# Unpacking double-precision weights beside an attention loop: three stages in three steps, integer mantissas, and another start

## The chip, the cores and the metric

One core of one Trainium2 chip. The metric is device time in microseconds (us) of one execution. The engines are PE (TensorE: matmuls), PEld (its weight loads), DVE (VectorE), ACT (ScalarE), POOL (GpSimd) and SP (SyncE, which starts the transfers). In these traces an engine works through its own instructions in program order (the prediction shows ACT standing for 3.77 us with a ready exponential behind it), and engines wait for one another by semaphores. "Granted clock" is the share of full speed that the chip's throttle gave PE.

## The reference

Attention in which a query sees only the keys with the same hash, then a feed-forward block with a squared ReLU:

```python
q_bits = (np.einsum('bhsd,dk->bhsk', q, proj) > 0)       # 4 x 8 heads, 768 tokens, 64 features, 6 bits
mask   = q_bucket[:, :, :, None] == k_bucket[:, :, None, :]
scores = np.where(mask, scale * q @ k.T, -1e9)
attn   = exp(scores - max); attn /= sum(attn) + 1e-9
x      = (attn @ v) as (3072, 512)
out    = np.maximum(x @ w_in, 0)**2 @ w_out              # w_in 512 x 2048, w_out 2048 x 512
```

The two weight matrices reach the kernel as 64-bit floating-point numbers. The kernel takes them apart with integer operations and puts fp32 numbers together.

## The kernel before

There are two stages. The attention stage works on 16 pairs of heads; a pair takes six steps, here called k0 to k5, one for each block of 128 keys. In each step PE makes scores in two sets of PSUM banks, ACT takes the exponential (which frees the banks), DVE adds the exponentials up, and PE multiplies the exponentials of an earlier step by the values ("attend"). Between these stands the preparation of the next pair: DVE transposes the queries (k1) and the keys (k2), PE hashes both (k3), ACT takes the signs (k3, k4). The product stage is the feed-forward block. The weights, in 32 pieces of 128 x 512, are converted during the attention stage, two pieces for each pair.

```python
    def part_weight(i):                                    # before
        high = raws[i][:, :, 1]
        nc.vector.tensor_scalar(out=power, in0=high, scalar1=20, scalar2=0x7FF,
            op0=ALU.logical_shift_right, op1=ALU.bitwise_and)
        nc.vector.tensor_scalar(out=top, in0=high, scalar1=3, scalar2=0x7FFFFF,
            op0=ALU.logical_shift_left, op1=ALU.bitwise_and)
        nc.scalar.activation(out=small, in_=power, func=ACTF.Relu, bias=excess)
        nc.scalar.activation(out=power, in_=small, func=ACTF.Copy, scale=2.0**23)
        nc.scalar.activation(out=one, in_=top, func=ACTF.Copy, scale=2.0**-23, bias=1.0)
    def round_weight(i): ...                               # three DVE operations over two tensors
    ...
        w_early.setdefault(u + (second if close else 2 * second), []).append((part_weight, i))
        w_steps.setdefault(u + (2 if close else SB - 1) + second, []).append((round_weight, i))
    ...
        for u in range(len(steps) + 1):
            for f, i in w_early.get(u, ()): f(i)           # ahead of the step's work
            add_up(*steps[u - 1])
            score(pr, kt)                                  # PE scores, then ACT's exponentials
            # ... spread, hash_bits, signs, weigh, attend, sum_up, normalize
            # ... features: DVE transposes q (k1) or k (k2) of the next pair
            for f, i in w_steps.get(u, ()): f(i)           # after it
```

So the two DVE operations and the three ACT operations on a piece are issued ahead of the step's exponentials.

## Time and profile before

| | before |
|---|---|
| median time | 1004.67 us (three runs) |
| span of the profiled run | 1002.8 us |
| first score matmul / first product matmul | 14.9 / 417.3 us |
| period of an undisturbed pair, hash to hash | 24.35 to 24.37 us |
| DVE / ACT busy in one pair | 17.4 / 17.2 us |

The lines on which the reading rests are shown inside the prediction below. One line of the page's fifth part (the costliest groups) belongs with them. Its columns are line, engine, operation, what is written and read with shapes, count, then busy us and mean ns, then the idle time of the engine just before this group and what ended it:

```profile
L147 ACT ACTIVATE small<-power,excess 128x512 uint8<-128x512 uint32 x32 | 23.1, 722 | 66.0 <-DVE power L137 65.9
```

The 23.1 us of work are not remarkable; the 66.0 us that ACT stood before it are. Idle time of an engine costs nothing unless something needed stands behind it, and here the exponentials do.

### The profile page before, as it was taken

What the parts mean: (1) busy time and instruction counts of PE and PEld (TensorE: products, weight loads), DVE (VectorE), ACT (ScalarE), POOL (GpSimd) and SP (SyncE); (2) the same over time, 40 slices, a digit from 0 to 9 for tenths busy, and PEclk for the clock granted to TensorE, in tenths of its full rate; (3) what the DMA queues carried; (4) which work ended last, traced back from release to release, by engine and by line L of the source; (5) the groups of instructions that cost most, each with busy time, mean ns of one, the idle gap of its engine ahead of it and who ended that gap; (6) DMA issues with size and microseconds to landing.
All of it is one profiled execution on the core that took longest, in us unless ns stands there. A gap on an engine that the chain in (4) does not pass through costs nothing.

```text
span 1002.8 us, 12978 instructions
## 1 busy us (share of the span) xinstructions
PE 941.5 (94%) x5166; PEld 656.1 (65%) x5166; DVE 555.6 (55%) x1074; ACT 390.0 (39%) x721; POOL 6.0 (1%) x22
## 2 busy tenths in 40 slices
PE   5888888888888888999999999999999999999998
PEld 2333333333333333588888888888888888888886
DVE  2677767777777777697028604840583068306600
ACT  5777667676766666232013102310221022002200
POOL 2000000000000000000000000000000000000000
PEclk8999999999999999999999999999999999999999
DMA  9454444454545521001022102210221021100000
GB/s 188 93 118 106 105 105 107 105 143 110 148 106 124 129 74 38 17 0 42 22 69 63 58 22 69 64 58 22 84 63 42 22 87 61 53 25 8 1 22 24
DMA packets 121155, 70.12 MB, mean 70 GB/s; under 512 B 99328, under 2 KB 104448, under 8 KB 121088
## 3 DMA queue, kind: packets, MB, share of 16 engines
q1 hardware_dynamic: 121024, 69.22, 26.4%
q8 instruction: 42, 0.69, 0.3%
q14 instruction: 25, 0.20, 0.1%
q0 software_dynamic: 64, 0.00, 0.0%
HBM read 54.53 MB, written 14.68 MB: 69 GB/s over the span
## 4 chain that ended last, share of the span: by engine, by line
PE 61%; DVE 1%; ACT 1%; issue 0%; DVEq 0%; ACTq 0%
PE acc L579 58%; PE xo L367 2%; PE st L339 1%; PE tot L385 0%; ACT e L344 0%; ACT small L147 0%; ACT power L148 0%; DVE flip L391 0%; ACT one L149 0%; DVE feat L281 0%; PE hash L294 0%; DVE power L137 0%; DVE w_out L166 0%; DVE one L163 0%; DVE power L159 0%
## 5 line engine op out<-in xcount | busy, mean ns | idle before, releaser
L579 PE MATMUL acc<-x,w_in 128*128 128x256 f32 x768 | 174.8, 379 | 0.0
L579 PE MATMUL acc<-w_out,g 128*128 128x256 f32 x768 | 168.7, 379 | 0.0
L344 ACT ACTIVATE e<-st 128x1024 f32<-128x1024 f32 x192 | 145.1, 806 | 54.4 <-PE st L339 52.5
L579 PEld LDWEIGHTS acc<-w_out,g 128*128 128x128 f32 x768 | 145.9, 190 | 19.8
L579 PEld LDWEIGHTS acc<-x,w_in 128*128 128x128 f32 x768 | 145.8, 190 | 19.8
L339 PE MATMUL st<-feat,feat 64*128 64x512 f32 (+1 forms) x768 | 154.9, 494 | 0.0
L367 PE MATMUL xo<-e,v_nat 128*64 128x512 f32 (+1 forms) x768 | 148.2, 507 | 4.6 <-DVE x_t L422 3.3
L579 PE MATMUL acc<-t_x,s_in 128*128 128x256 f32 x576 | 132.2, 379 | 0.0
L579 PE MATMUL acc<-t_out,gs 128*128 128x256 f32 x576 | 126.3, 379 | 0.0
L579 PEld LDWEIGHTS acc<-t_out,gs 128*128 128x128 f32 x576 | 109.5, 190 | 14.9
L579 PEld LDWEIGHTS acc<-t_x,s_in 128*128 128x128 f32 x576 | 109.4, 190 | 14.9
L367 PEld LDWEIGHTS xo<-e,v_nat 128*64 128x64 f32 x768 | 47.8, 139 | 95.7 <-issue 84.6
L339 PE MATMUL st<-bits,bits 64*128 64x256 bf16 (+1 forms) x384 | 65.0, 332 | 45.1 <-ACT e L344 40.1
L357 DVE TENSOR_TENSOR total<-total,e 128x1536 f32<-128x1536 f32 x48 | 84.3, 1757 | 32.7 <-ACT e L344 32.6
L339 PEld LDWEIGHTS <-bits 64*128 64x128 bf16 x384 | 20.6, 94 | 109.8 <-issue 108.7
L703 DVE TENSOR_TENSOR o<-acc,two 128x256 f32<-128x256 f32 x12 | 5.1, 424 | 156.7 <-PE acc L579 156.7
L339 PEld LDWEIGHTS st<-feat,feat 64*128 64x128 f32 x768 | 68.6, 193 | 34.5 <-issue 32.2
L673 DVE SCALAR_TENSOR_TENSOR g<-h 128x256 f32<-128x256 f32 x192 | 77.3, 423 | 4.9
L586 ACT COPY two<-acc 128x256 f32<-128x256 f32 x60 | 22.3, 372 | 143.4 <-PE acc L579 142.0
L304 ACT ACTIVATE bits<-hash,lifts 32x384 bf16<-32x384 f32 x120 | 68.6, 572 | 4.5 <-PE hash L294 2.7
L147 ACT ACTIVATE small<-power,excess 128x512 uint8<-128x512 uint32 x32 | 23.1, 722 | 66.0 <-DVE power L137 65.9
L672 DVE TENSOR_TENSOR h<-acc,two 128x256 f32<-128x256 f32 x48 | 20.3, 424 | 51.1 <-PE acc L579 51.1
(87 smaller groups left out, 626.4 us busy)
## 6 DMA issues: line engine op xcount, KB each, us to landing
raw<-in_moe_w_in_dram SPq DMA_DIRECT2D x16, 512.0 KB, 4.2
raw<-in_moe_w_out_dram SPq DMA_DIRECT2D x16, 512.0 KB, 3.7
v_nat<-in_v_dram SPq DMA_DIRECT2D x16, 384.0 KB, 3.9
x_all<-x_t SPq DMA_DIRECT2D x16, 384.0 KB, 2.7
x<-x_all SPq DMA_DIRECT2D x6, 1024.0 KB, 5.1
out_dram<-o SPq DMA_DIRECT2D x24, 256.0 KB, 2.0
raw_qk<-in_k_dram SPq DMA_DIRECT2D x16, 384.0 KB, 3.1
raw_qk<-in_q_dram SPq DMA_DIRECT2D x16, 384.0 KB, 3.3
```

The source lines that it names most:

```text
L147: nc.scalar.activation(out=small, in_=power, func=ACTF.Relu, bias=excess)
L304: nc.scalar.activation(out=t[h * D:h * D + NR_B, c * HS:(c + 1) * HS], in_=hashed[pr][h][at, 0:HS], func=ACTF.Sign, scale=HUGE, bias=lifts ...
L339: nc.tensor.matmul(out=st[:, h, 0:hi - lo], lhsT=src[pr, 1][rows, key], rhs=src[pr, 0][rows, lo:hi], start=first, stop=not first,)
L344: nc.scalar.activation(out=e[:, :, lo:hi], in_=st[:, :, 0:hi - lo], func=ACTF.Exp, scale=scale)
L357: nc.vector.tensor_tensor(out=totals[pr], in0=in0, in1=weights[pr, kt][:, :, 0:S], op=ALU.add)
L367: nc.tensor.matmul(out=xo[h * D:(h + 1) * D, lo:hi], lhsT=nat[pr, "v_nat"][:, h, kt * D:(kt + 1) * D], rhs=weights[pr, kt][:, h, lo:hi], s ...
L579: nc.tensor.matmul(out=acc[to], lhsT=a(i), rhs=b(i), start=first and i == 0, stop=last and i == n - 1, skip_group_check=True,)
L586: nc.scalar.copy(out=t, in_=acc[of])
L672: nc.vector.tensor_tensor(out=h, in0=one, in1=two, op=ALU.add)
L673: nc.vector.scalar_tensor_tensor(out=out, in0=h, scalar=0.0, in1=h, op0=ALU.max, op1=ALU.mult)
L703: nc.vector.tensor_tensor(out=out, in0=one, in1=two, op=ALU.add)
```

## The change

The intent is that ACT never waits for DVE. A piece now goes through three stages in three different steps: DVE takes it apart, ACT places the exponent in a later step and after that step's exponential, and DVE rounds in a step later still. The mantissa stays an integer until it is rounded, which saves one ACT operation on each piece. The sums over weights (all but the first) and over the first chunk of x move to the heads of steps. At the very start the first pair's key bits are made by comparisons on DVE instead of signs on ACT.

```diff
-        nc.vector.tensor_scalar(out=top, in0=high, scalar1=3, scalar2=0x7FFFFF, logical_shift_left, bitwise_and)
+        nc.vector.tensor_scalar(out=top, in0=high, scalar1=0xFFFFF, scalar2=0x100000, bitwise_and, bitwise_or)
+        parts[i] = power, top
+    def place_power(i):
         nc.scalar.activation(out=small, in_=power, func=ACTF.Relu, bias=excess)
         nc.scalar.activation(out=power, in_=small, func=ACTF.Copy, scale=2.0**23)
-        nc.scalar.activation(out=one, in_=top, func=ACTF.Copy, scale=2.0**-23, bias=1.0)
 ...  # round_weight: low * 2**-32 + top as integers; the last operation also scales by 2**-20
-        w_early ... part_weight;  w_steps ... round_weight
+        if i < 2:    at = i, 3 + i, 4 + i, 5 + i
+        elif second: at = max(u - 3, SB - 1), u + 1, u + 2, u + 4
+        else:        at = max(u - SB - 1, ...), u - 1, u, u + 3
+        for f, n in zip((load_weight, part_weight, place_power, round_weight), at):
+            w_steps.setdefault(n, []).append((f, i))
 ...  # sums_in, all but the first: from the end of a k3 to the head of a k0; sums_x: from the end of step 66 to the head of step 36
-        for w in (1, 0): signs(0, w)
-        weigh(0)
+        signs(0, 0)
+        first_keys()      # four comparisons and one multiply-add on DVE
```

(Argument lists are shortened and cuts are marked by "...".)

More of the change, by code (lines that the diff above doesn't have):

```diff
@@ L133, in part_weight @@
         power = p_w.tile([P, PIECE], U32, name="power")
-        small = p_w.tile([P, PIECE], U8, name="small")
-        one = p_w.tile([P, PIECE], FP32, name="one")
-        top = one.bitcast(U32)
+        top = p_w.tile([P, PIECE], U32, name="top")
         nc.vector.tensor_scalar(
@@ L141, in part_weight @@
         nc.vector.tensor_scalar(
-            out=top, in0=high, scalar1=3, scalar2=0x7FFFFF,
-            op0=ALU.logical_shift_left, op1=ALU.bitwise_and,
-        )
+            out=top, in0=high, scalar1=0xFFFFF, scalar2=0x100000,
+            op0=ALU.bitwise_and, op1=ALU.bitwise_or,
+        )
+        parts[i] = power, top
+    def place_power(i):
+        if i not in parts:
+            return
+        power = parts[i][0]
+        small = p_w.tile([P, PIECE], U8, name="small")
         nc.scalar.activation(out=small, in_=power, func=ACTF.Relu, bias=excess)
         nc.scalar.activation(out=power, in_=small, func=ACTF.Copy, scale=2.0**23)
-        nc.scalar.activation(out=one, in_=top, func=ACTF.Copy, scale=2.0**-23, bias=1.0)
-        parts[i] = power, one
     def round_weight(i):
@@ L157, in round_weight @@
         low, high = raw[:, :, 0], raw[:, :, 1]
-        power, one = parts.pop(i)
+        power, top = parts.pop(i)
         nc.vector.scalar_tensor_tensor(
@@ L162, in round_weight @@
         )
+        one = top.bitcast(FP32)
         nc.vector.scalar_tensor_tensor(
-            out=one, in0=low, scalar=2.0**-52, in1=one, op0=ALU.mult, op1=ALU.add,
+            out=one, in0=low, scalar=2.0**-32, in1=top, op0=ALU.mult, op1=ALU.add,
         )
-        nc.vector.tensor_tensor(
-            out=pieces[i][3], in0=one, in1=power.bitcast(FP32), op=ALU.mult
+        nc.vector.scalar_tensor_tensor(
+            out=pieces[i][3], in0=one, scalar=2.0**-20, in1=power.bitcast(FP32),
+            op0=ALU.mult, op1=ALU.mult,
         )
@@ L181 @@
     lifts = const.tile([P, 1], FP32, name="lifts")
+    spans = const.tile([P, 1], FP32, name="spans")
+    bases = const.tile([P, 1], FP32, name="bases")
     excess = const.tile([P, 1], FP32, name="excess")
@@ L196, in constants @@
             nc.gpsimd.dma_start(out=projs[h * D:(h + 1) * D, 0:N], in_=proj)
-        for t in (gains, lifts):
+        for t in (gains, lifts, spans, bases):
             nc.vector.memset(t, 0.0)
@@ L203, in constants @@
             nc.vector.memset(gains[r:r + N], FAR / 2)
+            nc.vector.memset(bases[r:r + N + 1], -FAR / 2 * N)
+            nc.vector.memset(bases[r:r + N], -FAR / 2)
+            nc.vector.memset(spans[r:r + N], FAR)
         for r in range(0, P, NR_B):
@@ L307, in signs, with first_keys @@
                 )
+    def first_keys():
+        bits[0, 1] = t = all_bits[0][1]
+        for c in range(2):
+            at = slice((2 + c) * NR_B, (3 + c) * NR_B)
+            for h in range(2):
+                nc.vector.tensor_scalar(
+                    out=t[h * D:h * D + NR_B, c * HS:(c + 1) * HS], in0=hashed[0][h][at, 0:HS],
+                    scalar1=0.0, scalar2=None, op0=ALU.is_gt,
+                )
+        nc.vector.tensor_scalar(
+            out=t, in0=t, scalar1=spans, scalar2=bases, op0=ALU.mult, op1=ALU.add
+        )
     def weigh(pr):
@@ L464 @@
         u, second = i // 2 * SB, i % 2
-        last = i // 2 == NP - 1
-        w_steps.setdefault(max(u - SB + (SB - 1) * second, i), []).append((load_weight, i))
         if i < 2:
-            u = SB // 2
-        close = last or i < 2
-        w_early.setdefault(u + (second if close else 2 * second), []).append((part_weight, i))
-        w_steps.setdefault(u + (2 if close else SB - 1) + second, []).append((round_weight, i))
-    W_IN = len(pieces) // 4 * SB + 1
-    for r in range(NR):
-        w_steps.setdefault(W_IN + r * SB + 2, []).append((sums_in, r))
-    X_0 = 5 * PB * SB // 2
+            at = i, 3 + i, 4 + i, 5 + i
+        elif second:
+            at = max(u - 3, SB - 1), u + 1, u + 2, u + 4
+        else:
+            at = max(u - SB - 1, (0, 2, SB)[i // 2] if i < 6 else 0), u - 1, u, u + 3
+        for f, n in zip((load_weight, part_weight, place_power, round_weight), at):
+            w_steps.setdefault(n, []).append((f, i))
+    W_IN = len(pieces) // 4 * SB - 1
+    for r in range(NR):
+        if r == 0:
+            w_steps.setdefault(W_IN + 4, []).append((sums_in, r))
+        else:
+            w_early.setdefault(W_IN + 1 + r * SB, []).append((sums_in, r))
+    X_0 = (PB + 1) * SB
     xs = {}
@@ L502 @@
         hash_bits(0, (st[:, 0], st[:, 1]))
-        for w in (1, 0):
-            signs(0, w)
-        weigh(0)
+        signs(0, 0)
+        first_keys()
         for u in range(len(steps) + 1):
@@ L509 @@
                 f(i)
+            if u == X_0 + SB:
+                sums_x(0)
             if 1 <= u <= len(steps):
@@ L549 @@
                 load_x(0)
-            if u == X_0 + SB:
-                sums_x(0)
         first.close()
```

## The prediction

> **What bounds the kernel now.** I read the page first: its engine shares and its 40 slices, then the list of waits, then the timeline of one repeat.
>
> ```profile
> PE 941.5 (94%) x5166; PEld 656.1 (65%) x5166; DVE 555.6 (55%) x1074; ACT 390.0 (39%) x721; POOL 6.0 (1%) x22
> ...
> PE   5888888888888888999999999999999999999998
> DVE  2677767777777777697028604840583068306600
> ACT  5777667676766666232013102310221022002200
> ```
>
> Two stages stand out. From slice 17 on (about 417 us, the first product matmul is at 417.3) PE has no gap; in the attention stage before it, it is eight tenths busy, while DVE and ACT stand at about seven. The change touches only the attention stage, so the last 1002.8 - 417.3 = 585.5 us should stay as they are, and the question is why PE idles in the first 417. The list of waits (engine and line, who it waited for, us in total, times, longest) answers:
>
> ```profile
> ACT small L147 <- DVE power L137: 65.9, 31, 6.3
> PE st L339 <- ACT e L344: 40.1, 18, 3.1
> PEld xo L367 <- DVE x_t L422: 10.2, 14, 3.0
> PE st L339 <- ACT bits L304: 4.9, 1, 4.9
> PE xo L367 <- DVE x_t L422: 3.3, 3, 2.6
> ```
>
> PE waits 18 times, 40.1 us, for an exponential, about once for each of the 16 head pairs. The first line hints at why the exponential is late: ACT itself has stood for 65.9 us before a weight-piece instruction. The timeline of one pair (start, duration, engine, line, what; in brackets the idle time before it) shows the order:
>
> ```profile
> 118.30 0.97 DVE L413 STREAM_TRANSPOSE recs<-tot 128x768 f32<-128x768 f32 x1
> 119.37 1.02 DVE L422 SCALAR_TENSOR_TENSOR x_t<-xo,recs 128x768 f32<-128x768 f32 x1
> 120.31 0.97 DVE L281 STREAM_TRANSPOSE feat<-q_nat 128x768 f32<-128x768 f32 x1
> 121.20 0.38 DVE L137 TENSOR_SCALAR power<-raw 128x512 uint32<-128x512 uint32 x1
> 121.62 0.72 ACT L147 ACTIVATE small<-power,excess 128x512 uint8<-128x512 uint32 x1 [3.77 <-DVE power L137]
> 122.38 0.63 ACT L148 ACTIVATE power<-small 128x512 uint32<-128x512 uint8 x1
> 122.91 0.61 ACT L149 ACTIVATE one<-one 128x512 f32<-128x512 uint32 x1
> 123.43 1.49 ACT L344 ACTIVATE e<-st 128x1024 f32<-128x1024 f32 x2
> 124.49 0.39 PE L339 MATMUL st<-bits,bits 64*128 64x512 bf16 x2 [2.52 <-ACT e L344]
> ```
>
> DVE comes to the piece's first operation only after the rounding of another piece, recs, x_t and the transposed queries. ACT meets the piece *ahead of* this step's exponential, stands 3.77 us, works 1.8 us, and only then starts the exponential that frees the score banks; PE is 2.52 us late. The scores had been ready since about 119.8 (they start at 118.54; with ACT idle the exponential follows 1.3 us later, as 116.34 does 115.04).
>
> **What the Trainium skill says.** "PSUM — Partial Sum Buffer", section Engine vs sequencer instructions, says that ScalarE and VectorE queues are strict first-in first-out. The lines above agree: a ready exponential stood 3.6 us behind a conversion. "TensorE: Matmul & The Clock Gate", Part 1, says that an idle PE falls to half its clock for a window of about 3.4 us. Here gaps of 2.5 us, shorter than the gap it warns of, do it sometimes:
>
> ```profile
> 100.14:124.49 24.35, 21.71 (x155) 8.72 (x155) 17.41 (x23) 17.17 (x27) 0.00 (x0) 1.00 0.48 108
> 124.49:150.41 25.92, 23.28 (x154) 9.13 (x154) 17.41 (x23) 17.27 (x27) 0.00 (x0) 0.93 0.45 102
> ```
>
> The columns after the length are the busy time of PE, PEld, DVE, ACT, POOL, then the granted clock. The same pair costs 1.57 us more at a mean clock of 0.93. "ScalarE: Activation LUTs", What ACT_TABLE_LOAD costs, gives 186 ns + 0.833 ns an element for an activation with immediates: 613 ns at 512 elements, and L149 takes 613 here. "VectorE: DVE Perf Modes", Mode 2×_2P, says that one-source fp32 operations in SBUF run at twice the rate of two-source ones: here 0.42 us for a TENSOR_SCALAR of 512 elements against 0.68 for a SCALAR_TENSOR_TENSOR.
>
> **The change, part by part.**
>
> *Busy time.* ACT loses the 32 activations of L149: 32 x 0.613 = 19.6 us. DVE keeps five operations for a piece of the same kinds and sizes (two of 0.42, three of 0.68; the last becomes a SCALAR_TENSOR_TENSOR, 0.684 instead of 0.692). None of this is on PE's path by itself.
>
> *Order.* I call the steps of a pair k0 to k5. The first piece of a pair is now taken apart on DVE at the end of the last pair's k5, placed on ACT after the exponential of k0, rounded at k3; the second at k1, k2 (after the exponential), k4. A walk through one pair, from the trace's durations with PE unhindered: k0 at 0; k1 at 4.60 (it has the total matmuls); k2 8.10; k3 11.27; k4 15.25 (hash matmuls, 0.81); k5 18.42; next pair 21.59. That is 6 x 3.17 (scores 1.72, attend 1.45) + 1.43 + 0.33 + 0.81.
> - ACT: an exponential starts 1.29 after its scores and may be up to 0.82 late before PE waits (PE follows its start by 1.06; 3.17 - 1.29 - 1.06 = 0.82). k0: exponential to 2.80, piece (0.72 + 0.63) to 4.15, next exponential due 5.89. k2: exponential to 10.90, piece to 12.25, next due 12.56. k3, k4: key and query signs of 2.33 each, as before; k5's exponential begins at 20.38, 0.67 late, inside the 0.82. No wait.
> - DVE at k1: without the rounding (which stood between 116.37 and 118.4), recs runs at 6.75 to 7.72 and x_t starts when attend ends, about 8.24, not 9.2 to 9.3 as now. The second piece's first operation ends at 10.5, before ACT is free at 10.90. x_t ends at 9.3, before the next attend at 9.82, so PE's small wait there goes too: k2 now takes 3.43 before the stall (118.54 to 121.97), 0.26 over 3.17. The sums of the x chunk move from k0 of a late pair, where they held x_t (PE waited 2.64), to the head of k0, where DVE has some 4 us free.
> - DVE at k3, k4: add and rounding 3.8 and, with weigh, 4.2 us against steps of 3.98 and 3.17; it catches up in k5 (total ready about 22.7, needed at 24.8).
>
> *Sum.* Of the 40.1 us: the start-up wait of 0.57 stays, and in the first pair (pieces in k3 and k4 beside both sign steps) I allow 1.2, for 38.3 saved. x_t: 14 x 0.26 + 2.6 = 6.2. Half clock: four pairs with 1.57, the last pair about 1.6, 7.9 together. Start: before the first score ACT does eight signs of 0.57 and PE waits 4.9; now four signs on ACT (2.3) beside four comparisons and one multiply-add on DVE (estimated 4 x 0.45 + 0.42 = 2.2 from DVE's 0.58 for 384 elements out of PSUM in flip and 0.42 for bits): 2.3 saved. Total 54.7, hence 950.
>
> **The rivals.**
> - *A new wait of PE for the keys' features.* DVE's second-step order is queries, piece, total, keys; by the walk the keys end at 13.35 and the second half of the hash needs them at 13.40. A DVE 0.3 us later costs 15 x 0.3 = 4.5 us. For it: no slack. Against: before, the stall hid it, and most of DVE's other work left these steps. I put in 3 us: 953.
> - *DVE becomes the bound.* It works 17.4 us a pair; with the four weight sums of 1.55 us in half the pairs, 19, against a period of 21.6. It binds only where k3 and k4 pile up: then the total or x_t would be late, perhaps 0.5 us a pair, 960.
> - *ACT is still late.* If pieces landed between signs and exponentials as in pair 0, 1.2 us a pair, 18 us, would stay: 970. The walk speaks against it, with 0.15 us of slack at k5.
> - *The loads are the hidden limit.* DMA is half busy and would have to bring the same bytes in 360 instead of 417 us; no PE or ACT wait names a load after the start, and q and k come two pairs ahead. Unlikely; 965 or more.
> - *Stage 1's saving is given back in the product stage.* PE has no gap there to fill or lose; against.
>
> **Range and chances.** With every wait gone and the full clock it would be about 947; with a quarter of the gain lost, 965. I say 953, from 947 to 963. Slower than 984.6 (2%) would need two thirds of the gain to vanish though the cause is plain in the trace: 0.96 for faster, 0.03 for same, 0.01 for slower.
>
> **What would show it.** In the changed profile: PE's wait for exponentials under 3 us; no long wait of ACT for DVE's power; the period of a pair 21.6 to 22 us against 24.36; granted clock 1.00 in every pair after the first; the first product matmul at 362 to 368 us; the stage behind it 585.5 us long. Waits of PE for feat (hash) or x_t would be the first rival; exponentials 0.8 us late after signs, the third. A stage two that is longer, or a pair period that stays above 23, would make the prediction wrong.

## The result

| | before | after |
|---|---|---|
| median time, same rounds | 1005.07 us | 959.44 us |
| ratio | | 0.9546 (95%: 0.9529 to 0.9562) |
| span of the profiled run | 1002.8 us | 956.8 us |
| first product matmul | 417.3 us | 370.7 us |
| product stage | 585.5 us | 586.1 us |
| period of an undisturbed pair | 24.36 us | 21.93 to 21.96 us |
| mean granted clock | 0.988 | 0.995 |

The time lies in the predicted range, 6.4 us above its centre. All of the gain is in the attention stage, which is 46.6 us shorter; the product stage is 0.6 us longer. The page of the changed kernel, its engine totals and slices:

```profile
PE 936.7 (98%) x5166; PEld 653.6 (68%) x5166; DVE 553.7 (58%) x1086; ACT 372.9 (39%) x685; POOL 6.0 (1%) x22
...
PE   5999999999999999999999999999999999999997
DVE  2677778778888886970287028702870187016600
ACT  4777777777777772320131013201320132013200
```

PE's eights have become nines from the second slice on. Three lines of the list of waits (engine and line, who it waited for, us in total, times, longest):

```profile
PE st L363 <- DVE bits L329: 5.4, 1, 5.4
PEld hash L304 <- DVE feat L291: 3.8, 14, 0.8
PE st L363 <- ACT e L368: 1.9, 2, 1.4
```

ACT's wait for DVE's exponents has gone from 65.9 to 0.3 us (one wait), and PE's wait for exponentials from 40.1 to 1.9 us: now ACT waits for PE's scores, 79 times and 89.5 us in all, as it should when PE is the bound. Two of the lines are new. At the start PE waits 5.4 us for DVE's key bits (before: 4.9 us for ACT's). And 14 times the weight load of the hash waits for DVE's transposed features. The timeline of one pair, around the place of the old stall (start, duration, engine, line, what, with the idle time before it in brackets):

```profile
133.01 1.02 DVE L446 SCALAR_TENSOR_TENSOR x_t<-xo,recs 128x768 f32<-128x768 f32 x1 [0.47 <-PE xo L391]
133.96 0.97 DVE L291 STREAM_TRANSPOSE feat<-q_nat 128x768 f32<-128x768 f32 x1
134.85 0.39 DVE L135 TENSOR_SCALAR power<-raw 128x512 uint32<-128x512 uint32 x1
135.48 1.75 DVE L381 TENSOR_TENSOR total<-e,e 128x1536 f32<-128x1536 f32 x1
135.60 0.72 ACT L152 ACTIVATE small<-power,excess 128x512 uint8<-128x512 uint32 x1
137.15 0.97 DVE L291 STREAM_TRANSPOSE feat<-k_nat 128x768 f32<-128x768 f32 x1
137.79 0.15 PEld L304 LDWEIGHTS hash<-feat,projs 64*32 64x32 f32 x8 [0.33 <-issue]
137.79 1.24 PE L304 MATMUL hash<-feat,projs 64*32 64x384 f32 x16
138.17 0.16 PEld L304 LDWEIGHTS hash<-feat,projs 64*32 64x32 f32 x8 [0.23 <-DVE feat L291]
138.96 1.51 PE L391 MATMUL xo<-e,v_nat 128*64 128x512 f32 x8
```

ACT takes the piece at once and then waits 0.38 us for the scores. The hash starts at 137.79 and the next work of PE at 138.96, 1.17 us later; before it was 0.80 (275.48 to 276.28 in a pair of the old trace). The weight loads of the hash in that old pair show the difference:

```profile
275.48 0.18 PEld L294 LDWEIGHTS hash<-feat,projs 64*32 64x32 f32 x16 [0.33 <-issue]
```

There all 16 loads went out within 0.18 us, and 8 of the 16 matmuls started within the first 0.06 us: the half for the queries and the half for the keys ran side by side. In the changed kernel 8 loads go out at 137.79 and 4 matmuls start in the first 0.06 us; the 8 loads of the key half follow only at 138.17, after DVE has written the keys' features (137.15 to 138.12). The halves run one after the other, and that is 0.36 us more. A whole pair in the changed kernel (after the length: busy time of PE, PEld, DVE, ACT, POOL, then the granted clock):

```profile
137.79:159.72 21.93, 21.93 (x156) 8.71 (x154) 19.52 (x28) 16.26 (x25) 0.00 (x0) 1.00 0.53 120
```

PE counts as busy for the whole period although it is 0.36 us longer than it need be: half of a hash is work too, and of the wait only the 0.23 us before the second weight loads show, as idle PEld. This pair also holds the sums of x; in an ordinary one (93.91 to 115.85) DVE is busy for 17.0 us, and in the fullest pair looked at (with a sum of weights) for 19.9. The clock is 1.00, and it is 1.00 over the whole stretch from 50 to 365 us.

### The profile page after: what moved, and what is told of

It reads as the page before. It is cut to its first block, busy times and chain, and to the rows that moved or that the text cites. A ratio compares the mean times of both kernels' runs of the same rounds, so it can differ in the third digit from the quotient of the medians.

```text
span 956.8 us, 12947 instructions
## 1 busy us (share of the span) xinstructions
PE 936.7 (98%) x5166; PEld 653.6 (68%) x5166; DVE 553.7 (58%) x1086; ACT 372.9 (39%) x685; POOL 6.0 (1%) x22
## 4 chain that ended last, share of the span: by engine, by line
PE 96%; DVE 1%; ACT 1%; DMA 0%; issue 0%; SPq 0%; DVEq 0%; ACTq 0%
PE acc L607 61%; PE st L363 17%; PE xo L391 14%; PE tot L409 2%; PE hash L304 2%; PE tot L433 1%; ACT bits L314 0%; ACT e L368 0%; DMA q_nat<-in_q_dram 0%; PE tp L281 0%; DVE bits L325 0%; DVE feat L291 0%; DVE total L381 0%; PE st L304 0%; DVE flip L415 0%
## 5 line engine op out<-in xcount | busy, mean ns | idle before, releaser
L368 ACT ACTIVATE e<-st 128x1024 f32<-128x1024 f32 x192 | 145.5, 810 | 90.0 <-PE st L363 89.5
L363 PE MATMUL st<-feat,feat 64*128 64x512 f32 (+1 forms) x768 | 151.7, 487 | 0.0
L391 PE MATMUL xo<-e,v_nat 128*64 128x512 f32 (+1 forms) x768 | 144.9, 498 | 0.2 <-DVE x_t L446 0.2
L607 PEld LDWEIGHTS acc<-t_out,gs 128*128 128x128 f32 x576 | 109.4, 190 | 14.9
L607 PEld LDWEIGHTS acc<-t_x,s_in 128*128 128x128 f32 x576 | 109.4, 190 | 14.9
L614 ACT COPY one<-acc 128x256 f32<-128x256 f32 x60 | 22.4, 373 | 67.3 <-PE acc L607 67.3
```

The source lines that it names most:

```text
L363: nc.tensor.matmul(out=st[:, h, 0:hi - lo], lhsT=src[pr, 1][rows, key], rhs=src[pr, 0][rows, lo:hi], start=first, stop=not first,)
L368: nc.scalar.activation(out=e[:, :, lo:hi], in_=st[:, :, 0:hi - lo], func=ACTF.Exp, scale=scale)
L391: nc.tensor.matmul(out=xo[h * D:(h + 1) * D, lo:hi], lhsT=nat[pr, "v_nat"][:, h, kt * D:(kt + 1) * D], rhs=weights[pr, kt][:, h, lo:hi], s ...
L607: nc.tensor.matmul(out=acc[to], lhsT=a(i), rhs=b(i), start=first and i == 0, stop=last and i == n - 1, skip_group_check=True,)
L614: nc.scalar.copy(out=t, in_=acc[of])
```

## The experiments

Eleven runs in three groups; the runs of a group share the runs of the kernel before (medians 1005.04, 1005.06 and 1005.66 us). The time of a group's kernels is compared with that of the changed kernel run again, 959.43 us. That run and the rest of the first group (a_banks, a_featk, a_both) were on one chip and the other two groups on another; the kernel before differs by 0.6 us between them. "Wait" and "period" are from the profile of each run.

| run | median us | ratio to before | period us | what it is |
|---|---|---|---|---|
| a_same | 959.43 | 0.954 | 21.94 | the changed kernel again |
| a_banks | 957.36 | 0.9517 | 21.94 | key hash of the first pair in its own PSUM banks |
| a_featk | 954.06 | 0.9487 | 21.58 | keys transposed before adding up |
| a_both | 950.75 | 0.9457 | 21.58 | both edits |
| a_start | 959.45 | 0.9527 | 21.94 | old start |
| a_arith | 959.64 | 0.953 | 21.94 | old arithmetic, three activations |
| a_sums | 960.47 | 0.9543 | 21.94 | sums in their old steps |
| a_round | 969.79 | 0.9633 | 22.65 | second rounding in its old place |
| b_place | 974.65 | 0.9683 | 22.65 | before, ACT's part of a piece after the exponential |
| b_ints | 995.60 | 0.9881 | 23.84 | before, new arithmetic only |
| a_best | 949.72 | 0.944 | 21.58 | a_both, first two pieces in other steps |

### a_same: the changed kernel again

No edit.

> The changed kernel once more, unaltered, as the base for the three beside it: 958 to 960 us, period of a pair 21.94 us (hash to hash), first score at about 15.4 us.

959.43 us (958.87 to 960.19), period 21.94. First score 15.55 us.

### b_place: only ACT's place in the order

```diff
-        nc.scalar.activation(...)  x3, inside part_weight
+    def place_weight(i): the same three activations
         w_early.setdefault(n, []).append((part_weight, i))
+        w_steps.setdefault(n, []).append((place_weight, i))    # same step, after the exponential
```

> The kernel before with one thing altered: ACT's three instructions on a piece are issued after the step's exponential instead of ahead of it; arithmetic, DVE's order and start as before. Theory (the exponential stood behind the piece in ACT's queue): PE's waits for exponentials fall from 40 us to under 5, the half clock goes, and the keys become what the hash waits for: period about 22.6, 968 to 974 us. Rival (ACT's freed time or the new steps are needed): 990 or more.

974.65 us: 31.0 us of the 45.6 come from this one edit, with the old arithmetic, the old start, and DVE's order of operations unchanged. Two of its waits:

```profile
PEld hash L302 <- DVE feat L289: 10.7, 14, 0.8
PE st L347 <- ACT e L352: 3.9, 3, 2.5
```

The exponentials' 40.1 us are down to 3.9 us, and the hash now waits for the features, by more than in the changed kernel (10.7 against 3.8 us). The time is 0.65 us above the range expected: the first pair's wait is 2.5 us here, and the pair with the sums of x lasts 25.19 us, 2.54 more than its neighbours, because those sums still hold x_t. These two pairs (the first lasts 25.49 us against 23.28 in the changed kernel) and the place of the rounding (a_round, 10.4 us) account for about 15.1 of the 15.2 us that still separate this run from the changed kernel.

### b_ints: only the arithmetic

```diff
-        nc.scalar.activation(out=one, in_=top, func=ACTF.Copy, scale=2.0**-23, bias=1.0)
+        # top stays an integer; round_weight as in the changed kernel; every step as before
```

> The kernel before with the new arithmetic alone: two activations on a piece instead of three, in the old place ahead of the exponential. Theory: the stall is shorter by the activation left out, 0.61 us a pair, so PE's wait is 1.9 instead of 2.52 us and the time 9.2 us less, 995.5; down to 988 if gaps of 1.9 us no longer bring the half clock. Rival (less work on ACT is the main gain): 980 or less.

995.60 us, as the theory had it, though in part by luck: the wait shrank by less than expected, and fewer dips of the clock made up for it.

```profile
ACT small L146 <- DVE power L136: 66.5, 31, 6.3
PE st L339 <- ACT e L344: 31.7, 18, 2.6
```

ACT stands as long as before, 66.5 us. PE's wait in a pair is 2.01 instead of 2.52 us, 0.51 less and not the 0.61 expected: in the old trace the exponential started 0.52 us after this activation (122.91 to 123.43), since the two overlap. All waits for exponentials together fall by 8.4 us (40.1 to 31.7). The half clock is rarer. In the kernel before it followed 3 of the 13 gaps of 2.52 us (one of the three had a gap of 0.47 us just before it); here it follows 1 of 13 gaps of 2.01 us. In both kernels it also came with each longer gap after the start (2.64 and 3.13 us; 2.65 and 2.61 here), but in b_place a gap of 2.65 us brought none. It varies between runs: one of the four runs here took 991.93 us at a mean clock of 0.995, the others 995.5 to 995.9 at 0.989.

### a_arith: the order without the arithmetic

```diff
+        nc.scalar.activation(out=top.bitcast(FP32), in_=top, func=ACTF.Copy, scale=2.0**-23, bias=1.0)
         # in place_power; the masks and the rounding as before
```

> The changed kernel's order with the arithmetic of before: the third activation on each piece is back, 32 x 0.613 = 19.6 us more work for ACT. Theory (only where the pieces stand in ACT's order matters): within 1 us of the changed kernel, about 960, as ACT has 0.8 us of room. Rival (ACT's load matters): 0.6 us a pair, 968 or more.

959.64 us, 0.2 from the changed kernel. The third activation costs ACT 19.6 us and the kernel nothing that these runs can tell; only in the first pair is PE's wait longer, 1.88 instead of 1.36 us. Together with b_place and b_ints this settles which part of the change does the work: the order. Less work for ACT is worth 10 us in the old order and nothing measurable in the new one.

### a_round: the second rounding back in its old place

```diff
-            at = max(u - 3, SB - 1), u + 1, u + 2, u + 4
+            at = max(u - 3, SB - 1), u + 1, u + 2, u + (SB if i // 2 < NP - 1 else 4)
         # the two copies of weights that are kept for later go out one step later, as they need the rounding
```

> The changed kernel with the second piece's rounding back at its old place, between the reciprocals and recs. Theory (x_t, queries, piece, total, keys, hash are one chain on DVE and the hash waits for its end): x_t 0.72 us later, and nearly all of it lands on PE, period 22.5 to 22.7, 968 to 970. Rival (only the small wait of attend for x_t comes back): 0.26 us a pair, 963.

969.79 us, period 22.65, 0.71 more than the changed kernel; the delay of x_t (it starts 16.71 us after the first attend that follows a hash, against 15.99) reaches PE whole: 0.53 us at the hash and 0.19 us before the next attend, which waits for x_t, so the rival names a part of it. At the hash:

```profile
PEld hash L304 <- DVE feat L291: 10.7, 14, 0.8
```

It is the same wait, the same total and the same period as in b_place, whose DVE order at k0 to k2 is the same. So the chain rounding, recs, x_t, queries, piece, sum, keys, hash sets the pair's period in these two runs. In the changed kernel the rounding is not in it: x_t waits there for PE (0.47 us in the lines above), and the chain begins with x_t.

### a_featk: the keys before the sum

```diff
+            keys_first = u < len(steps) and steps[u][1] == 2 and steps[u][0] + 1 < NP
+            if keys_first:
+                features(steps[u][0] + 1, 1)
             if 1 <= u <= len(steps):
                 add_up(*steps[u - 1])
```

> In the third step of a pair DVE transposes the next pair's keys before it adds up, not after. Theory (the second half of the hash waits for the keys, about 0.35 us in each of 14 pairs): the period falls from 21.94 to 21.59 us and the time by 4.9 us, to about 954.5. Rival (the 0.35 us is another cost, or the sum that is now later makes PE wait): less than 1 us.

954.06 us, 5.4 less, and 21.58 for every pair after the first. The wait is gone from its list of waits. One pair of it:

```profile
133.56 0.97 DVE L291 STREAM_TRANSPOSE feat<-k_nat 128x768 f32<-128x768 f32 x1
134.46 1.72 DVE L381 TENSOR_TENSOR total<-e,e 128x1536 f32<-128x1536 f32 x1
135.87 0.87 PE L304 MATMUL hash<-feat,projs 64*32 64x384 f32 x16
```

The keys are ready 1.3 us before the hash starts (133.56 + 0.97 against 135.87), and the 16 matmuls count 0.87 us instead of 1.24. The sum, now 0.9 us later, has room. The gain is what the periods say: 13 x 0.36 and one pair with 0.89, 5.6 us.

### a_start: the old start

```diff
-        signs(0, 0)
-        first_keys()
+        for w in (1, 0):
+            signs(0, w)
+        weigh(0)
```

> The changed kernel with the start of before: key and query signs both on ACT, then the weighing. Theory (the new start gains nothing, since DVE waits for ACT): first score at 14.9 instead of 15.4 us, and the time 0.4 us under the changed kernel, 959.0. Rival (the new start does save 2.3 us, as predicted): 2.3 us slower, 961.7.

959.45 us. PE's wait before the first score is 4.92 us as in the kernel before, against 5.36 in the changed kernel. The expected 0.4 us is below the spread of the runs (958.47 to 960.40), so the time only excludes that the new start saves 2.3 us; the wait shows that it saves nothing. (The first score itself is no measure between runs: here it came at 15.93 and not at 14.9, and PE had waited 0.73 us for the first keys to land, which it does not in the kernel before.)

### a_banks: the key hash in banks of its own

```diff
-        st = score_banks(0)
-        hash_bits(0, (st[:, 0], st[:, 1]))
+        st, sk = score_banks(0), score_banks(1)
+        hash_bits(0, (st[:, 0], st[:, 1]), (sk[:, 0], sk[:, 1]))    # queries, keys
```

> The first pair's key hash goes to PSUM banks of its own, so that DVE's comparisons need not wait for ACT's query signs. Theory (DVE waited because both read one PSUM tile): the comparisons run beside the signs, the first score starts at about 12.7 us instead of 15.4, and the whole is 2.7 us shorter than the changed kernel, about 956.7. Rival (something else held them, or PE's half clock at the start eats it): first score still after 15, or the time within 0.5 us of the changed kernel.

957.36 us, 2.1 less. The start of the changed kernel:

```profile
10.11 2.33 ACT L314 ACTIVATE bits<-st,lifts 32x384 bf16<-32x384 f32 x4 [0.99 <-PE st L304]
12.54 2.27 DVE L325 TENSOR_SCALAR bits<-st 32x384 bf16<-32x384 f32 x4 [9.83 <-ACT bits L314]
15.37 0.61 PE L363 MATMUL st<-bits,bits 64*128 64x512 bf16 x2 [5.36 <-DVE bits L329]
```

and of this one:

```profile
10.06 2.33 ACT L315 ACTIVATE bits<-st,lifts 32x384 bf16<-32x384 f32 x4 [1.04 <-PE st L305]
10.69 2.27 DVE L326 TENSOR_SCALAR bits<-st 32x384 bf16<-32x384 f32 x4 [7.99 <-PE st L305]
13.53 0.39 PE L364 MATMUL st<-bits,bits 64*128 64x512 bf16 x2 [2.97 <-DVE bits L330]
```

In the changed kernel the comparisons begin when ACT's signs end (the releaser in brackets is ACT), and in this one they run beside them (the releaser is PE). In the first case both engines read one PSUM tile, and the program makes the second reader wait for the first. The wait falls from 5.36 to 2.97 us, 2.4 us; the first score came at 13.5 instead of the expected 12.7 us. The comparisons start 0.63 us after the signs, when PE has finished the key hash, and the four of them (2.27 us) and the multiply-add (0.48 us) stand before the score.

### a_both: both edits

> Both edits. Theory: the two add up, 7.6 us under the changed kernel, about 951.8; first score at 12.7 us and period 21.59 us. Rival: they overlap, or a third wait takes their place, 954 or more.

950.75 us, 8.7 less than the changed kernel; the sum of the two single gains, 2.1 and 5.4, is 7.5, and the spread of the runs is 1 to 2. They add up, and no third wait came.

### a_sums: the sums in their old steps

```diff
-    W_IN = len(pieces) // 4 * SB - 1;  X_0 = (PB + 1) * SB;  sums_in and sums_x at the heads of k0
+    W_IN = len(pieces) // 4 * SB + 1;  X_0 = 5 * PB * SB // 2;  both at the ends of steps
```

> The changed kernel with the weight sums and the sums of x in their old steps. Theory: one long hold of x_t by the sums of x, 1 to 2.6 us, and nothing from the weight sums: 960.5 to 962. Rival (the sums' places mattered in each of their eight pairs): 965 or more.

960.47 us, 1.0 slower, which the spread hardly separates from nothing. The profile is clearer: two pairs last 22.72 and 22.46 instead of 21.94 us, 1.3 us in all, and PE waits 0.72 us for x_t once; the pairs that hold a weight sum keep their 21.94.

### a_best: the first two pieces in other steps

```diff
-            at = i, 3 + i, 4 + i, 5 + i
+            at = i, 2 + 2 * i, 2 + 3 * i, 5 + i     # on top of a_both
```

> Both edits of a_both, and in the first pair the first piece is taken apart and placed one step earlier and the second placed one step later, so that no piece stands beside a sign step. Theory: PE's 1.36 us wait for an exponential in the first pair goes, about 950.5 against 951.8 without it. Rival: the wait moves to the next step, 951.8 or more.

949.72 us (949.50 to 951.50), ratio 0.944. The first pair's wait of 1.36 us is not in its profile, and the first period falls from 23.28 to 21.87. It is the fastest kernel of this study, 9.7 us under the change and 56 us under the kernel before, and its outputs are correct.

## Why the prediction was right, and by how much it was off

The prediction was right in its range and in its main mechanism. Step by step, in its order:

- **PE's wait for exponentials, 38.3 us to be saved.** It went from 40.1 to 1.9 us. b_place shows that the cause was the place in ACT's queue. The work taken from ACT gives 8.4 us of this wait by itself in the old order (b_ints) and nothing measurable in the new one (a_arith).
- **The smaller waits for x_t, 6.2 us.** PEld's wait for x_t fell from 10.2 to 0.6 us and PE's from 3.3 to 0.2. The walk through a pair gave 21.59 us for a PE that nothing hinders; a_featk and a_both run at 21.58. a_round shows that the place of the rounding was part of it: 0.71 us a pair comes back with it. The one large hold, by the sums of x, is worth less in the changed order than the 2.6 us counted (a_sums: 1.3).
- **The half clock, 7.9 us.** It is gone: the clock is 1.00 from 50 to 365 us, and the kernel before had five dips of 3.4 us in its attention stage (at 125, 224, 296, 351 and 398 us). That the gaps cause the dips is supported by b_place, which has no dip after the first 30 us, and by b_ints, where shorter gaps bring fewer; it is not shown, as no run changed the gaps alone and a gap of 2.65 us in b_place brought no dip.
- **"Start: ... now four signs on ACT (2.3) beside four comparisons", 2.3 us to be saved.** This step failed. The two were not beside each other. The comparisons waited for the signs since both read one PSUM tile, and the start became 0.44 us longer (5.36 against 4.92). a_banks puts them side by side and gains 2.4 us of wait. Even so a comparison was mis-sized, 0.57 us for the 0.45 estimated, and the multiply-add with two column operands, 0.48 for 0.42.
- **The first rival, a new wait for the keys' features, allowed 3 us.** It is what happened, and it was mis-sized. The walk had the keys end at 13.35 and "the second half of the hash needs them at 13.40", and took that for no wait. The first time was right: in the trace the keys end 0.33 us after the hash starts (by the walk 13.35 against 11.27 + 1.72 = 12.99, 0.36 us). The need was wrong. When its operands are there the key half runs beside the query half, so the keys are needed when the hash starts, and their whole lateness is lost: 0.36 us in each pair, and 0.89 in the second, where the keys are 0.87 us late because DVE is still busy with the first pair's rounding. a_featk measures it as 5.4 us.
- **The other rivals.** DVE did not become the bound (17.0 us of 21.94 in an ordinary pair, 19.9 in the fullest looked at), ACT was late only in the first pair (1.36 us for the 1.2 allowed), no load was waited for, and the product stage kept its length (586.1 us against 585.5).
- **The signs that were named.** PE's wait for exponentials, the period and the clock came out as said; the first product matmul, at 370.7 us, is outside the 362 to 368 us.

The start (2.7 us worse than its term) and the keys (2.4 us more than allowed) make 5.1 of the 6.4 us between 953 and 959.4; the rest is not separated from the spread of the runs. The three terms before the start add up to 52.4 us. Not each, but their sum can be measured: from the first score to the first product matmul the changed kernel takes 355.3 us instead of 402.4, 47.0 less, and 52.6 with the 5.6 us that the keys cost. The sum without any allowance was 950, and with these two things mended a_both ran in 950.75.

## What to carry to other kernels

When an engine with in-order instructions does a side job, the place of that job among its main work counts for more than its length: here moving three instructions behind the exponential was worth 31 us, while removing one of them was worth 10 us in the old place and nothing measurable in the new one. When the largest wait goes, look at once at the chain that it was hiding, and give the instruction another engine needs first the first place on its engine. Two engines are side by side only if the program lets them be: look for what each of them waits on, down to a shared PSUM tile. And where the parts of one group run side by side, all their operands are needed when the group starts.

## What the Trainium skill lacked or had wrong

- "TensorE: Matmul & The Clock Gate", Part 1: the page ties the fall to half clock to idle gaps of about 3.4 us. Here 3 of 13 gaps of 2.52 us were followed by a dip that cost 1.57 us, and 1 of 13 gaps of 2.01 us in b_ints; in b_place a gap of 2.65 us was followed by none. The page gives no chance for gaps of such a length; of shorter ones it says only, for another kernel, that frequent micro-idling makes the clock oscillate.
- "PSUM — Partial Sum Buffer", PSUM bank collisions raise a hardware error: the page bars two engines from one bank in the same 32-partition quadrant. Here the two readers stood in different quadrants (query hashes in rows 0 to 63, key hashes in rows 64 to 127), and the program still made one wait for the other, 2.4 us. The page does not say that a guard by tile costs this; no run here tried the two reads in one bank without it.
